# One run of matmuls for a unit's scores and the preceding unit's outputs, with the second head's blocks in the opposite rows

## The chip, the cores and the metric

One core of a Trainium2 chip runs the kernel. The time is device microseconds from start to end of one execution. The kernel before takes 614.58 us, the median of 3 runs (613.74 to 617.41).

## What is computed

Attention with a decay, in blocks of 64 positions (B = 4, H = 8 heads, S = 768, D = 64), and behind it a feed-forward net with softplus (512 to 2048 to 512) on all 3072 positions, in float32:

```
for b in range(nb):                                    # blocks of 64
    intra = (qb @ kb.T * Dmask) @ vb                   # Dmask[i,j] = lam**(i-j), 0 above the diagonal
    inter = (qb * lam_pow) @ kv_state
    out[b] = intra + inter
    kv_state = lam_block * kv_state + (kb * rev_pow).T @ vb
x = out laid out as (B*S, 512)
return softplus(x @ w_in) @ w_out
```

## The kernel before

The order of all instructions is written out by hand (`manual_schedule`): each engine runs its own in the order of the program, and waits are put in where data or buffers need them.

**Units.** The sequence is cut into 6 chunks of 128 positions, that is two blocks (s = 0 and 1) of 64. A *unit* g is one chunk of one pair of heads (t = 0 and 1) for all four batches b: 4 units to a chunk, 24 in all. Its q, k, v come in one buffer `att{g}` (two DMAs on SP, `load_upto`, L80 to L85). In SBUF block s = 0 stands in rows (partitions) 0 to 63, `lo`, and s = 1 in rows 64 to 127, `hi`.

For a unit, TensorE does two blocks of small fp32 matmuls (64 x 64 each):
- *scores* (`mm_scores`, L289 to L304): per b, t and s one product of k and q into the PSUM bank x, in rows `half(s)` (L299), and one of the decayed keys kd and v, the *sum* that the state takes up, into the bank y, in rows `half(1 - s)` (L301). In the last chunk the sums of s = 1 are left out.
- *outputs* (`mm_out`, L307 to L321): per b, s and t one product of state and decayed q (L314) and one of v and masked scores a (L318), into rows `half(t)` of bank s of a PSUM tile.

Around them: `k_decay` (ACT, two instructions, L277), `q_decay` (POOL for units under 8, VectorE after them, L284), `mask_scores` (VectorE, x times mask, into a, L326), `update_states` (VectorE, four instructions L331: from the state of block 0 to that of block 1, and on to the unit of the next chunk), `x_high` (ACT, L363) and `x_low` (VectorE, L370), which split a unit's outputs into two parts for the net.

**The net.** Step s of 96 takes 128 of the 2048 hidden columns of one chunk: 16 steps to a chunk. `mlp1(s)` (L389 to L401) is 12 matmuls of 128x128x512 into one PSUM bank (`bank`, L70, tag h, two buffers). `chain_act` (ACT, softplus, L379), `chain_hi` (ACT, L383) and `chain_lo` (VectorE, L387) make two parts of it. `mlp2(s - 4)` (L403 to L423), again 12 matmuls, adds the step into four banks of output rows. All matmuls of the net are in two parts, three products each.

**Weights.** They come as 64-bit numbers, and in the first chunk each step converts one pair of tiles: on ACT `w_scale`, `w_round` (L205, L209), on VectorE `w_shift`, `w_sign`, `w_add` (L213, L217, L223), and one step later `w_hi` on ACT (L226) and `w_lo` on VectorE (L230). `mlp2(s - 4)` and `mlp1(s)` need what `w_lo` made in step s - 1.

**Order.** A prologue written as a list of words (L453 to L463) does units 0 to 3 and the scores of unit 4, and the first steps. Then the loop from L473: in step s first the decays of the unit that has scores in step s + 1, then the chain of step s - 1, the weights, `mlp2(s - 4)`, a scores block if the step has one (steps 6, 9 and 12 for units 5 to 7, then 17, 21, ... 77), an outputs block if it has one (5, 8, 11, 14 for units 4 to 7, then 19, 23, ... 79), `mlp1(s)`, loads of weights, and, in a step with scores, the load of the next unit.

**Buffers.** PSUM has 8 banks: 4 for outputs of the net, 2 for h, 2 for the tile of the attention blocks (`work`, L66). In SBUF one pool of 21 buffers of 8 KB per row (`t8`) holds weights, raw weights, units, x parts, the `spare` tile of the prologue and the output rows; a tile waits until one is free. kd, qd and a of a unit are 2 KB tiles (`t2`, 4 buffers).

Of the kernel before, what the change touches and what calls it, by code (L numbers as in the profile page):

```python
# [7 lines left out]
F32 = mybir.dt.float32  # L8
# [3 lines left out]
ALU = mybir.AluOpType  # L12
# [4 lines left out]
T = 64  # L17
# [9 lines left out]
def half(i):  # L27
    return slice(i * 64, (i + 1) * 64)
# [3 lines left out]
def decay_attention_softplus_ffn(  # L32
# [19 lines left out]
        return sb.tile(shape, dt, tag="b4", bufs=7, name=name)  # L52

    def t2(shape, dt, name):
        return sb.tile(shape, dt, tag="b2", bufs=4, name=name)

    def tl(shape, dt, name):
        return sb.tile(shape, dt, tag="bl", bufs=1, name=name)
# [1 line left out]
    def th(shape, dt, name):  # L60
        return sb.tile(shape, dt, tag="bh", bufs=5, name=name)
# [5 lines left out]

        return ps.tile([128, 2, 512], F32, tag="t", bufs=1, name=name)

    def bank(name):  # L70
        return ps.tile([128, 512], F32, tag="h", bufs=2, name=name)

# [12 lines left out]
    def part(g, major, kind):  # L87
        return units[g][:, major, kind].rearrange("q (b t d) -> q b t d", b=B, t=2)
# [7 lines left out]
    def kt_of(g):  # L96
        return part(g, 1, 0)

    def vt_of(g):
        return part(g, 1, 1)  # L100


    w_order = [(f, 0) for f in range(LAG)]
# [27 lines left out]
    spare = t8([128, 4, 512], F32, "spare")  # L131
    warm = t8([128, 512], F32R, "warm")
    nc.vector.memset(warm.bitcast(F32), 0.0)
    warm_ps = bank("warm_ps")

    def keep_warm(n):
        for _ in range(n):
# [40 lines left out]
    nc.gpsimd.iota(  # L178
        off[half(1)], pattern=[[1, T]], base=0, channel_multiplier=-1, allow_small_or_imprecise_dtypes=True
    )  # L180
    diag = cp.tile([128, H, T], F32, name="diag")
    nc.vector.scalar_tensor_tensor(
        out=diag[half(1)], in0=off[half(1)].rearrange("q (o i) -> q o i", o=1).broadcast_to([64, H, T]), scalar=0.0,
        in1=lam_c[half(1)].rearrange("q (h o) -> q h o", o=1).broadcast_to([64, H, T]),
# [65 lines left out]
    def heads(g):  # L250
        p = g % NP
        return slice(2 * p, 2 * p + 2)

    def first_chunk(g):
        return g < NP

    def last_chunk(g):
        return g >= NG - NP
# [10 lines left out]
    def k_decay(g):  # L269
        kd = kds[g] = own(g, 0, "kd")  # L270
        if g == 0:
            w = rp1[:, heads(g)].rearrange("q (o t w) -> q o t w", o=1, w=1).broadcast_to([128, B, 2, D])
            nc.vector.tensor_mul(out=kd, in0=kt_of(g), in1=w)
            return
        for t in range(2):
            h = heads(g).start + t
            nc.scalar.activation(kd[:, :, t], kt_of(g)[:, :, t], AF.Copy, scale=rp1[:, h : h + 1])  # L277

    def q_decay(g):
        qd = qds[g] = own(g, 1, "qd")  # L280
        r = hi if first_chunk(g) else slice(0, 128)
        eng = nc.gpsimd if g < 2 * NP else nc.vector
        w = lp[r, heads(g), :].rearrange("q (o t) i -> q o (t i)", o=1).broadcast_to([r.stop - r.start, B, 2 * T])
        eng.tensor_mul(  # L284
            out=qd[r].rearrange("q b t i -> q b (t i)"), in0=q_of(g)[r].rearrange("q b t i -> q b (t i)"), in1=w
        )


    def mm_scores(g, x, y):  # L289
        q, k, kd, v = q_of(g), k_of(g), kds.pop(g), vt_of(g)  # L290
        if first_chunk(g):

            nc.tensor.matmul(y[lo], lhsT=warm[hi, :64], rhs=warm[hi], start=True, stop=False)
        for b in range(B):
            for t in range(2):
                cols = slice((2 * b + t) * 64, (2 * b + t + 1) * 64)
                for s in range(2):
                    r = half(s)
                    nc.tensor.matmul(x[r, cols], lhsT=k[r, b, t], rhs=q[r, b, t], start=True, stop=True)  # L299
                    if s == 0 or not last_chunk(g):  # L300
                        nc.tensor.matmul(  # L301
                            y[half(1 - s), cols], lhsT=kd[r, b, t], rhs=v[r, b, t],
                            start=s == 0 or not first_chunk(g), stop=s == 0 or not first_chunk(g),
                        )  # L304


    def mm_out(g, w):  # L307
        a, qd, v, st = aa.pop(g), qds.pop(g), vt_of(g), states[g]
        for b in range(B):
            cols = slice(b * 64, b * 64 + 64)  # L310
            for s in range(1 if first_chunk(g) else 0, 2):
                r = half(s)
                for t in range(2):
                    nc.tensor.matmul(w[half(t), s, cols], lhsT=st[r, b, t], rhs=qd[r, b, t], start=True, stop=False)  # L314
            for s in range(2):
                r = half(s)
                for t in range(2):
                    nc.tensor.matmul(  # L318
                        w[half(t), s, cols], lhsT=v[r, b, t], rhs=a[r, b, t],
                        start=s == 0 and first_chunk(g), stop=True,  # L320
                    )  # L321

    def mask_scores(g, x):
        a = aa[g] = own(g, 2, "a")
        m = mask[:, heads(g), :].rearrange("q (o t) i -> q o t i", o=1).broadcast_to([128, B, 2, T])
        nc.vector.tensor_mul(out=a, in0=x.rearrange("q (b t i) -> q b t i", b=B, t=2), in1=m)  # L326

    def decayed(g, to, of, r, u):
        for t in range(2):
            h = heads(g).start + t  # L330
            nc.vector.scalar_tensor_tensor(  # L331
                out=to[:, :, t], in0=of[:, :, t], scalar=lam_c[r, h : h + 1], in1=u[:, :, t],
                op0=ALU.mult, op1=ALU.add,
            )


    def first_states(g, y):
# [10 lines left out]
            )  # L348

    def next_states(g, y):  # L350
        nc.scalar.copy(out=states[g][lo].rearrange("q b t d -> q (b t d)"), in_=y[lo])

    def update_states(g, y):
        u = y.rearrange("q (b t e) -> q b t e", b=B, t=2)
        st = states[g]
        decayed(g, st[hi], st[lo], lo, u[hi])
        if not last_chunk(g):
            states[g + NP] = th([128, B, 2, D], F32, f"st_{g + NP}")
            decayed(g, states[g + NP][lo], st[hi], hi, u[lo])

    def x_high(g, w):

# [26 lines left out]
    def mlp1(s, ps_=range(NP)):  # L389
        c, f = divmod(s, NF)  # L390
        if s not in h_tiles:
            h_tiles[s] = bank(f"h{s}")
        w = w_of(f, 0)
        for p in ps_:
            cs = slice(p * 128, (p + 1) * 128)
            x = x_of(c, p)
            for n, (i, j) in enumerate(((0, 0), (1, 0), (0, 1))):
                nc.tensor.matmul(  # L398
                    h_tiles[s], lhsT=w[:, i, cs], rhs=x[:, j, :],
                    start=p == 0 and n == 0, stop=p == NP - 1 and n == 2,  # L400
                )  # L401

    def mlp2(ss):  # L403
# [6 lines left out]
        for b in range(B):  # L410
# [8 lines left out]
            if ends:  # L419
# [2 lines left out]
                queue = nc.scalar if c == NCH - 1 and b % 2 == 0 else nc.sync  # L422
                queue.dma_start(out=out[b * S + c * C : b * S + (c + 1) * C, :], in_=ob[:, b])  # L423

    def w_group(j):
        return (2 * j, 2 * j + 1) if 2 * j < NW else ()

    def scores_of(g):
        w = work(f"w{g}")
        mm_scores(g, w[:, 0], w[:, 1])  # L430
        mask_scores(g, w[:, 0])
        update_states(g, w[:, 1])


    xy, z = {}, {}
# [29 lines left out]
        step[name](*map(int, numbers))  # L465

    last = NCH * NF
    scores_at = {3 * n + 3: NP + n for n in range(NP)}  # L470
    scores_at.update({4 * n + 1 + NF: 2 * NP + n for n in range(NG - 2 * NP)})
    outs_at = {s + 2: g for s, g in scores_at.items()}
    for s in range(LAG, last + LAG):  # L473
        if s + 1 in scores_at:
            k_decay(scores_at[s + 1])
            q_decay(scores_at[s + 1])
        if s - 1 < last:
            chain_act(s - 1)
            chain_hi(s - 1)
            chain_lo(s - 1)  # L480
        old, new = w_group(s - 1), w_group(s)
        if old:
            w_hi(*old)
        if new:
            w_scale(*new)
            w_round(*new)
        if old:
            w_lo(*old)
        if new:
            w_shift(*new)  # L490
            w_sign(*new)
            w_add(*new)
        if s == last + LAG - 2:
            mlp2([s - LAG, s - LAG + 1])
        elif s - LAG < last - 1:
            mlp2([s - LAG])
        if s in scores_at:
            scores_of(scores_at[s])
        if s in outs_at:
            g = outs_at[s]  # L500
            w = work(f"z{g}")
            mm_out(g, w)
            x_high(g, w)
            x_low(g, w)
        if s < last:
            mlp1(s)
        w_load(2 * s + (8 if s < 9 else 6))
        if s in scores_at:
            load_upto(scores_at[s] + 2)


def _layout(q, k, v, lam, w_in, w_out):
    import numpy as np


    def split(a, back):
        a = a.reshape(B, NP, 2, NCH, 2, T, D).transpose(3, 1, 0, 2, 4, 5, 6)
        return a[:, :, :, :, :, ::-1] if back else a

    qs, ks, vs = split(q, False), split(k, True), split(v, True)  # L520

    dmaj = [a.transpose(0, 1, 4, 6, 2, 3, 5) for a in (qs, ks)]
    tmaj = [a.transpose(0, 1, 4, 5, 2, 3, 6) for a in (ks, vs)]
    att = np.stack([a.reshape(NCH, NP, 128, 512) for a in dmaj + tmaj], axis=3)
    att = np.ascontiguousarray(att).reshape(NCH, NP, 128, 2, 2, 512)
    wi = w_in.reshape(NP, 128, NF, 128).transpose(2, 1, 0, 3).reshape(NF, 1, 128, DM)
    wo = w_out.reshape(NF, 1, 128, DM)
    wts = np.ascontiguousarray(np.concatenate([wi, wo], axis=1)).view(np.int64)
    return att, np.ascontiguousarray(lam), wts
# [20 lines left out]
```

## Time and profile before

| | us |
|---|---|
| median of 3 runs | 614.58 (613.74 to 617.41) |
| the profiled execution | 615.21 |
| its span, first to last instruction | 613.4 |
| TensorE busy in it | 603.6 |
| VectorE, ACT busy in it | 227.0, 211.9 |

The profile is of one execution. Its rows give start and duration in microseconds on each engine; L with a number is a line of the kernel before. A row of the timeline joins neighbours of one kind (x12: twelve instructions, the duration being that of all together). PE is TensorE's matmuls, PEld its weight loads, DVE is VectorE, ACT is ScalarE, POOL is GpSimd, SP issues DMAs. What stands in brackets behind a row is the idle time of the engine before it and who ended it.

### The profile page before, as it was taken

How to read it: one execution, taken by the hardware profiler on the slowest of the kernel's cores; microseconds unless marked ns; L12 is line 12 of the kernel's file. 1: busy time of each engine (PE TensorE's matmuls, PEld its weight loads, DVE VectorE, ACT ScalarE, POOL GpSimd, SP SyncE). 2: the span in 40 equal slices, each digit the busy share in tenths (PEclk: the TensorE clock that was granted, in tenths of full speed). 3: DMA queues.
4: the chain of work that ended last, by engine and by line, in shares of the span. 5: the costliest groups of instructions: out<-in, count | busy, mean ns of one | idle time of the engine just before them, and what ended most of it. 6: DMA issues, size and time to landing. Idle time of an engine off the chain costs nothing.

```text
span 613.4 us, 11764 instructions
## 1 busy us (share of the span) xinstructions
PE 603.6 (98%) x5289; PEld 488.9 (80%) x5289; DVE 227.0 (37%) x330; ACT 211.9 (35%) x340; POOL 13.5 (2%) x17
## 2 busy tenths in 40 slices
PE   9899999999999999999999999999999999999997
PEld 6577778888888888888888888888888888888886
DVE  7679999843232223223213322222222211210111
ACT  3677677623222223132223231312312322322121
POOL 3200000000000000000000000000000000000000
PEclk9889999999999999999999999999999999999999
DMA  8995224213010032120030320002302000100001
GB/s 297 406 407 217 96 92 138 73 67 138 9 63 1 1 138 93 45 69 2 1 138 13 126 70 1 2 25 114 138 1 71 1 0 1 69 2 0 1 0 68
DMA packets 15169, 48.98 MB, mean 80 GB/s; under 512 B 1808, under 2 KB 1808, under 8 KB 15120
## 3 DMA queue, kind: packets, MB, share of 16 engines
q1 hardware_dynamic: 14832, 47.72, 21.3%
q8 instruction: 41, 0.67, 0.4%
q10 hardware_dynamic: 288, 0.52, 0.2%
q14 instruction: 8, 0.07, 0.0%
HBM read 41.95 MB, written 6.29 MB: 79 GB/s over the span
## 4 chain that ended last, share of the span: by engine, by line
PE 91%; DVE 3%; DMA 2%; ACT 1%; issue 1%; SPq 1%; POOL 0%; ACTq 0%; DVEq 0%
PE h L398 42%; PE o L415 41%; PE w L299 3%; PE z L314 2%; PE z L318 2%; DMA att<-in_att 2%; DVE w L230 1%; DVE st L331 1%; PE w L301 1%; DVE g L387 0%; ACT l L379 0%; ACT w L226 0%; DVE a L326 0%; SPq L84 0%; POOL own L284 0%
## 5 line engine op out<-in xcount | busy, mean ns | idle before, releaser
L398 PE MATMUL h<-x,w 128*128 128x512 f32 x1152 | 284.9, 396 | 0.0
L415 PE MATMUL o<-w,g 128*128 128x512 f32 x1152 | 277.1, 389 | 1.3 <-DVE w L230 1.3
L415 PEld LDWEIGHTS o<-w,g 128*128 128x128 f32 x1152 | 216.0, 188 | 47.3 <-DVE w L230 2.6
L398 PEld LDWEIGHTS h<-x,w 128*128 128x128 f32 x1152 | 213.9, 189 | 47.7 <-issue 0.8
L387 DVE TENSOR_TENSOR g<-l,g 128x512 fp32r<-128x512 f32 x96 | 66.4, 691 | 284.7 <-ACT g L383 284.6
L379 ACT ACTIVATE l<-h 128x512 f32<-128x512 f32 x96 | 57.3, 597 | 305.2 <-PE h L398 302.5
L383 ACT CAST g<-l 128x512 fp32r<-128x512 f32 x96 | 59.6, 621 | 3.1
L331 DVE SCALAR_TENSOR_TENSOR st<-st,lam_c,w 64x256 f32<-64x256 f32 x72 | 31.7, 479 | 0.8
L370 DVE TENSOR_TENSOR x<-z,x 128x512 fp32r<-128x512 f32 x24 | 16.6, 690 | 38.4 <-ACT x L363 38.4
L363 ACT CAST x<-z 128x512 fp32r<-128x512 f32 x24 | 14.0, 584 | 40.4 <-PE z L318 40.4
L299 PEld LDWEIGHTS w<-att 64*64 64x64 f32 x640 | 20.4, 134 | 7.0 <-issue 6.0
L326 DVE TENSOR_TENSOR a<-w,mask 128x512 f32<-128x512 f32 x20 | 13.8, 691 | 29.7 <-PE w L301 22.4
L299 PE MATMUL w<-att 64*64 64x64 f32 x640 | 23.1, 221 | 0.0
L301 PE MATMUL w<-att,kd 64*64 64x64 f32 x576 | 23.0, 221 | 0.0
L277 ACT ACTIVATE kd<-att,rp 128x256 f32<-128x256 f32 x40 | 18.1, 504 | 14.1 <-DMA att<-in_att 14.1
L230 DVE TENSOR_TENSOR w<-c,w 128x1024 fp32r<-128x1024 f32 (+1 forms) x19 | 21.1, 1112 | 4.7 <-ACT w L226 4.7
L314 PEld LDWEIGHTS z<-qd,st 64*64 64x64 f32 x640 | 17.0, 134 | 7.0 <-issue 7.0
L226 ACT CAST w<-c 128x1024 fp32r<-128x1024 f32 (+1 forms) x19 | 17.4, 914 | 15.0 <-DVE c L223 12.4
L205 ACT ACTIVATE c<-raw 128x1024 f32<-128x1024 f32 (+1 forms) x19 | 19.0, 999 | 7.4 <-DMA raw<-in_wts 7.4
L223 DVE CUSTOM_DVE_ANT_0 c<-raw,c 128x2048 uint16<-128x2048 uint16 (+1 forms) x19 | 20.1, 1057 | 2.4
L314 PE MATMUL z<-qd,st 64*64 64x64 f32 x640 | 20.9, 224 | 0.0
L301 PEld LDWEIGHTS w<-att,kd 64*64 64x64 f32 x576 | 20.3, 134 | 0.0
(47 smaller groups left out, 210.6 us busy)
## 6 DMA issues: line engine op xcount, KB each, us to landing
att<-in_att SPq DMA_DIRECT2D x48, 512.0 KB, 5.2
raw<-in_wts SPq DMA_DIRECT2D x32, 512.0 KB, 10.2
out_dram<-ob SPq DMA_DIRECT2D x22, 256.0 KB, 2.1
out_dram<-ob ACTq DMA_DIRECT2D x2, 256.0 KB, 2.0
lam_b<-in_lam SPq DMA_DIRECT2D x1, 4.0 KB, 2.6
```

Source lines behind the costliest of these rows:

```text
L205: nc.scalar.activation(c.bitcast(F32), raw_at(ks, 1).bitcast(F32), AF.Copy, scale=2.0**-112)
L223: nc.vector.tensor_add(out=c, in0=c, in1=raw_at(ks, 0))
L230: nc.vector.tensor_sub(out=w[:, 1], in0=conv.pop(ks[0]).bitcast(F32), in1=w[:, 0])
L299: nc.tensor.matmul(x[r, cols], lhsT=k[r, b, t], rhs=q[r, b, t], start=True, stop=True)
L301: nc.tensor.matmul(y[half(1 - s), cols], lhsT=kd[r, b, t], rhs=v[r, b, t], start=s == 0 or not first_chunk(g), stop=s == 0 or not first_ch ...
L314: nc.tensor.matmul(w[half(t), s, cols], lhsT=st[r, b, t], rhs=qd[r, b, t], start=True, stop=False)
L331: nc.vector.scalar_tensor_tensor(out=to[:, :, t], in0=of[:, :, t], scalar=lam_c[r, h : h + 1], in1=u[:, :, t], op0=ALU.mult, op1=ALU.add,)
L379: nc.scalar.activation(l_tiles[s], h_tiles.pop(s), AF.Softplus)
L383: nc.scalar.copy(out=g_tiles[s][:, 0, :], in_=l_tiles[s])
L387: nc.vector.tensor_sub(out=g[:, 1, :], in0=l_tiles.pop(s), in1=g[:, 0, :])
L398: nc.tensor.matmul(h_tiles[s], lhsT=w[:, i, cs], rhs=x[:, j, :], start=p == 0 and n == 0, stop=p == NP - 1 and n == 2,)
L415: nc.tensor.matmul(o_tiles[c][b], lhsT=g[:, i, b * 128 : (b + 1) * 128], rhs=w[:, j], start=f == 0 and n == 0, stop=f == NF - 1 and n == 2,)
```

## The change

A unit's scores and sums and the outputs of the unit before it are done in one function, `mm_both`, as one run of small matmuls: all outputs first, then `mm_sums`. There are 19 such runs (units 5 to 23: steps 6, 9, 12, 15, then 19, 23, ... 75); outputs of unit 23 remain a block of their own in step 79. Scores go into a bank of their own (tag z); the sums stand in columns 256 to 511 of the two banks in whose columns 0 to 255 the outputs are. From the second chunk on, the two blocks of the second head (t = 1) are stored in the opposite rows: `row(g, t, n)` says in which rows block n is. h has one buffer, and steps of `in_z` take the bank z for h instead. A copy of v (`keep_values`) lets a unit's buffer go before its outputs are done. `diag` moves into a part of `spare`, and its place goes to a fifth `t2` buffer.

```diff
-        return sb.tile(shape, dt, tag="b2", bufs=4, name=name)
+        return sb.tile(shape, dt, tag="b2", bufs=5, name=name)
-    def bank(name):
-        return ps.tile([128, 512], F32, tag="h", bufs=2, name=name)
+    def bank(name, tag):
+        return ps.tile([128, 512], F32, tag=tag, bufs=1, name=name)
+    def keep_values(g):
+        v = t2([128, B, 2, D], F32, f"v_{g}")
+        nc.scalar.copy(out=v, in_=part(g, 1, 1))
+        values[g] = v
-    diag = cp.tile([128, H, T], F32, name="diag")
+    diag = begins[0]
+    def row(g, t, n):
+        return n if first_chunk(g) else n ^ t
...
     def mm_scores(g, x, y):
...
+        u = y.rearrange("q (b t e) -> q b t e", b=B, t=2)
+        sums[g] = {(t, n): u[half(1 - row(g, t, n)), :, t] for t in range(2) for n in range(2)}
+        mm_sums(g, x, q, k, kd, v)
+
+    def mm_sums(g, x, q, k, kd, v):
         for b in range(B):
             for t in range(2):
                 cols = slice((2 * b + t) * 64, (2 * b + t + 1) * 64)
                 for s in range(2):
-                    r = half(s)
+                    r, n = half(s), row(g, t, s)
                     nc.tensor.matmul(x[r, cols], lhsT=k[r, b, t], rhs=q[r, b, t], start=True, stop=True)
-                    if s == 0 or not last_chunk(g):
...
+                    if n == 0 or not last_chunk(g):
+                        whole = n == 0 or not first_chunk(g)
+                        nc.tensor.matmul(sums[g][t, n][:, b], lhsT=kd[r, b, t], rhs=v[r, b, t], start=whole, stop=whole)
...
+    def mm_both(g, x, w):
+        q, k, kd, v = q_of(g), k_of(g), kds.pop(g), vt_of(g)
+        a, qd, vo, st = aa.pop(g - 1), qds.pop(g - 1), vt_of(g - 1), states[g - 1]
+        y = sums[g] = {}
+        for t in range(2):
+            for n in range(2):
+                s = row(g, t, n)
+                o = w[half(s), 0] if t else w[half(1 - s), 1]
+                y[t, n] = o[:, 256:512].rearrange("q (b e) -> q b e", b=B)
+        for b in range(B):
+            cols = slice(b * 64, (b + 1) * 64)
+            for n, (left, right) in enumerate(((st, qd), (vo, a))):
+                for s in range(2):
+                    r = half(s)
+                    for t in range(2):
+                        nc.tensor.matmul(
+                            w[half(t), row(g, t, s), cols], lhsT=left[r, b, t], rhs=right[r, b, t],
+                            start=n == 0, stop=n == 1,
+                        )
+        mm_sums(g, x, q, k, kd, v)
...
     def next_states(g, y):
-        nc.scalar.copy(out=states[g][lo].rearrange("q b t d -> q (b t d)"), in_=y[lo])
+        u = y[lo].rearrange("q (b t e) -> q b t e", b=B, t=2)
+        for t in range(2):
+            nc.scalar.copy(out=states[g][half(row(g + NP, t, 0)), :, t], in_=u[:, :, t])
...
+            h_tiles[s] = bank(f"h{s}", "z" if s in in_z else "h")
...
+    both_at = {3 * n + 6: NP + 1 + n for n in range(NP)}
+    both_at.update({4 * g - 17: g for g in range(2 * NP + 1, NG)})
+    in_z = {1, 3, 5} | {s + 1 for s in both_at} | {s - 1 for s in both_at if s > NF}
...
+        if s in both_at:
+            g = both_at[s]
+            w, xb = work(f"w{g}"), bank(f"x{g}", "z")
+            mm_both(g, xb, w)
+            x_high(g - 1, w)
+            x_low(g - 1, w)
+            mask_scores(g, xb)
+            update_states(g)
+            if NP + 1 < g < NG - 1:
+                keep_values(g)
+        if s == 4 * NG - 17:
+            zw = work(f"z{NG - 1}")
+            mm_out(NG - 1, zw)
+            x_high(NG - 1, zw)
+            x_low(NG - 1, zw)
         if s < last:
             mlp1(s)
         w_load(2 * s + (8 if s < 9 else 6))
-        if s in scores_at:
-            load_upto(scores_at[s] + 2)
+        if s in both_at:
+            load_upto(both_at[s] + 2)
...
     def split(a, back):
-        a = a.reshape(B, NP, 2, NCH, 2, T, D).transpose(3, 1, 0, 2, 4, 5, 6)
+        a = a.reshape(B, NP, 2, NCH, 2, T, D).transpose(3, 1, 0, 2, 4, 5, 6).copy()
+        a[1:, :, :, 1] = a[1:, :, :, 1, ::-1].copy()
```

`update_states` keeps its four VectorE instructions per unit, now on `sums[g]` and with rows by `row`; `mm_out` has the same products as before with `row` for the bank.

## Rows read from the trace of the kernel before

**Rows 1.** The page, parts 1 (busy us) and 2 (tenths in 40 slices)
```profile
PE 603.6 (98%) x5289; PEld 488.9 (80%) x5289; DVE 227.0 (37%) x330; ACT 211.9 (35%) x340; POOL 13.5 (2%) x17
...
DVE  7679999843232223223213322222222211210111
...
PEclk9889999999999999999999999999999999999999
```

**Rows 2.** TensorE's waits, 115 to 600 us: total, times, longest
```profile
PEld z L314 <- issue: 5.6, 16, 0.4
PEld w L299 <- issue: 5.6, 16, 0.4
```

**Rows 3.** TensorE's timeline around an output block: start, duration, what
```profile
106.34 2.88 PE L398 MATMUL h<-x,w 128*128 128x512 f32 x12
109.06 2.88 PE L415 MATMUL o<-w,g 128*128 128x512 f32 x12
...
112.04 0.30 PE L318 MATMUL z<-a,att 64*64 64x64 f32 x8
...
112.74 0.30 PE L318 MATMUL z<-a,att 64*64 64x64 f32 x8
112.97 3.02 PE L398 MATMUL h<-x,w 128*128 128x512 f32 x12
115.82 2.88 PE L415 MATMUL o<-w,g 128*128 128x512 f32 x12
```

**Rows 4.** TensorE's timeline, first passes of a scores block
```profile
129.51 0.27 PE L299 MATMUL w<-att 64*64 64x64 f32 x1
129.52 0.27 PE L301 MATMUL w<-att,kd 64*64 64x64 f32 x1
129.53 0.27 PE L299 MATMUL w<-att 64*64 64x64 f32 x1
129.53 0.27 PE L301 MATMUL w<-att,kd 64*64 64x64 f32 x1
```

**Rows 5.** TensorE's timeline in the prologue, outputs of unit 3
```profile
30.10 0.28 PE L318 MATMUL z<-own,att 64*64 64x64 f32 x4
30.22 0.28 PE L314 MATMUL z<-own,st 64*64 64x64 f32 x4
```

**Rows 6.** VectorE's timeline, steps 7 to 10
```profile
68.53 0.69 DVE L387 TENSOR_TENSOR g<-l,g 128x512 fp32r<-128x512 f32 x1
...
74.69 1.23 DVE L230 TENSOR_TENSOR w<-c,w 128x1024 fp32r<-128x1024 f32 x1 [0.51 <-ACT w L226]
...
79.06 0.68 DVE L370 TENSOR_TENSOR x<-z,x 128x512 fp32r<-128x512 f32 x1
...
81.46 1.79 DVE L213 TENSOR_SCALAR c<-c 128x1024 uint32<-128x1024 uint32 x1
...
85.80 0.68 DVE L326 TENSOR_TENSOR a<-w,mask 128x512 f32<-128x512 f32 x1
...
88.31 0.69 DVE L387 TENSOR_TENSOR g<-l,g 128x512 fp32r<-128x512 f32 x1
```

**Rows 7.** TensorE's timeline, steps 8 to 12
```profile
70.41 2.79 PE L415 MATMUL o<-w,g 128*128 128x512 f32 x11 [0.53 <-DVE w L230]
...
79.89 0.27 PE L299 MATMUL w<-att 64*64 64x64 f32 x1
...
86.56 2.88 PE L398 MATMUL h<-x,w 128*128 128x512 f32 x12
...
99.67 0.27 PE L299 MATMUL w<-att 64*64 64x64 f32 x1
...
100.77 3.02 PE L398 MATMUL h<-x,w 128*128 128x512 f32 x12
```

**Rows 8.** ACT's groups: busy us, mean ns, idle us before them and its end
```profile
L379 ACT ACTIVATE l<-h 128x512 f32<-128x512 f32 x96 | 57.3, 597 | 305.2 <-PE h L398 302.5 <-DVE g L387 2.6
...
L421 ACT COPY ob<-o 128x512 f32<-128x512 f32 x12 | 7.0, 586 | 9.2 <-PE o L415 9.2
```

## What I expect

> **What bounds the kernel now.** I read the page first, parts 1 and 2: TensorE is busy for 603.6 of 613.4 us, and its granted clock is full (tenths of 9, that is the 2.4 GHz level) from the fourth slice on; VectorE is full only in slices 4 to 7, about 46 to 107 us [rows 1]. A busy TensorE is not TensorE at its peak, so I read its waits next: between 115 and 600 us it waits for no other engine at all; the only rows are 0.35 us of its own issue, 16 times ahead of an output block and 16 times ahead of a scores block [rows 2]. So in four fifths of the span the end is set by what TensorE issues, and by nothing else. Third came TensorE's timeline. A layer run (12 matmuls of mlp1 or mlp2) takes 109.06 - 106.34 = 2.72 us. An output block stands between two of them: from the start of the run ahead of it to the start of the run behind it are 112.97 - 109.06 = 3.91 us, and that run then takes 2.85 [rows 3]. The block costs (3.91 - 2.72) + (2.85 - 2.72) = **1.32 us**. A scores block has as many products and costs the same: 100.77 - 99.67 = 1.10 us from its first pass to the next layer run [rows 7], and 1.09 in an output block. Fourth, VectorE's timeline for the stage where it is full, below.
>
> **Inside a block.** The 32 fp32 products of a block show as 64 passes, two each (L318 x8 where the code issues four). Four neighbours start within 0.02 us of each other: they are on four different quarters of the array, named here by input half and output half, 00, 01, 10, 11 [rows 4]. From L318 of b = 0 to L318 of b = 3 are 12 passes on each quarter: (112.74 - 112.04) / 12 = 0.0583 us a pass [rows 3]. Is that the price of a pass on one quarter, or of four passes through something they share? [rows 5] tells: in the prologue only the two quarters of one input half have work (four passes of L318, then four of L314, two on each), and 30.22 - 30.10 = 0.12 us go by for two passes each, again 0.06. So a quarter takes one pass in 0.058 us, whatever the other three do. So a block costs its fixed part plus the passes of its fullest quarter. Now that is 16 passes, 0.933 us; fixed part 1.32 - 0.933 = **0.387 us** (the first pass, and the change to and from whole-array matmuls).
>
> **The change, part by part.** *One run in place of two blocks.* 19 runs (units 5 to 23) and one last output block replace 19 scores and 20 output blocks; 19 fixed parts go, 19 x 0.387 = 7.35 us, were the passes the same. *But the quarters are no longer even.* In mm_both the outputs stay two per quarter and b: t goes to output half t. The sums don't: for head 0 they land in half(1-s), opposite the scores; for head 1 in half(s), the very quarter in which x[r] gets its scores. Per b, quarters 00 and 11 then have three products of mm_sums and 01 and 10 have one. The fullest has 4 x (2 + 3) = 20 products, 40 passes, 40 x 0.0583 = 2.333 us; a run costs 0.387 + 2.333 = **2.72 us**, against 2.64 for the two blocks. (In the last chunk, with n = 0 alone, quarter 11 still has three.) The merge loses 0.08 us each time. Bounds, since no row shows such a run: if only the total of passes counted, 0.387 + 32 x 0.0583 = 2.25; if products could start only in the program's order, one product more in the run, 2.84. I take 2.72, for [rows 5] is the nearest case: a part of the quarters in use, the pace unchanged.
>
> *The first stage, up to step 15.* Here VectorE decides [rows 6]. Its period of three steps, from one L387 after the states to the next, is 88.31 - 68.53 = 19.78 us; TensorE's, scores to scores, is 99.67 - 79.89 = 19.78 too [rows 7], though its own work is 6 x 2.72 + 2 x 1.32 = 18.96: the missing 0.82 is the wait of mlp2 at 70.41 for w_lo (L230). So what TensorE saves or pays here shows only through VectorE. VectorE's instructions stay (the long shift L213 of 1.79 us too), but their order doesn't: x_low (0.68 us at 79.06) moves from a step of its own into that of mask and states. Each step's L230 waits for ACT's w_hi, which waits for w_add; an attention operation in between covers this. Now only one step in three is uncovered (0.51 at 74.69); after it two are. Period 19.78 + 0.5 = 20.3. Nor is that the only place: bank z has the scores until mask_scores has read them, and then mlp1(s + 1). The mask ended at 85.80 + 0.68 = 86.48, mlp1(10) began at 86.56 [rows 6, 7]; with x_low ahead and 0.5 lost, the mask is 1.1 to 1.2 late and mlp1(10), which comes 0.7 later than now, waits some 0.4 us. This I count at nothing, since mlp2 behind it would have waited for L230 that long. If mask and w_lo didn't overlap so, it is the rival below.
>
> The run at step 6 begins 1.0 us earlier than scores(5) now (no output block at step 5: 1.32, less 0.3 for L230); two periods cost 0.5 each; so the run of unit 7 begins at about 99.7, as scores(7) do now, 99.67 [rows 7]. But unit 6's outputs, done by then before, are still in it. From here TensorE is the bound in both. Left before: 17 scores and 17 output blocks, 34 x 1.32 = 44.88 us. Left after: 17 x 2.72 + 1.32 = 47.56. Difference **+2.7 us**.
>
> *Costed at nothing, and what hides it.* keep_values: 17 copies on ACT at about 0.59 us (the copy of L421) beside 305 us in which ACT waits for mlp1 [rows 8]; uncovered, 10 us. With one bank each, h and z alternate; where two neighbours share h (steps 8 and 9, 77 to 95), mlp1 needs chain_act of the step before, 0.60 us, and has an mlp2 of 2.72 us to hide it. next_states: 4 copies become 8 half ones in the prologue, at most 4 x 0.6 more on ACT; I take 0 and keep 2 for the range. diag in begins[0] holds spare's buffer longer, while loads run far ahead: 0, up to 1. x_high now waits for the whole run, sums included; behind it on ACT stand keep_values and chain_act(s), whose mlp1 is only done 2.7 us later. Scores of a unit come two steps earlier, and its load_upto with its two DMAs on SP too, at steps 35, 51 and 67 now behind four output DMAs; a load still has three steps, over 16 us, until k_decay asks for it, and the copied values free its buffer sooner: 0.
>
> Sum on the profiled execution: 615.2 + 2.7 = 617.9; it was 0.6 above the median of the runs, so 617.3 against 614.58, +0.4%.
>
> **A rule that speaks against it.** In [rows 4] the two L299 products, from opposite input halves, write one bank and start 0.02 us apart. The Trainium skill, TensorEngine Tiling (Array Packing), Gotcha 1: PSUM Pressure, says that different row tiles cannot access the same PSUM bank at once. The trace disagrees with it. By that rule the new outputs, in which both input halves write each bank, would take turns: 16 passes more in 20 places, 18.7 us, and the time would be 636.
>
> **Rivals.** *Even pace* (only the number of passes counts): runs of 2.25, left after step 12 39.6 instead of 44.88, 609.3 us. For it: four quarters have only been seen evenly loaded; against it: [rows 5]. *VectorE's stage heals*: buffers come free earlier, so the waits like that at 70.41 go (there are three, at most 2.5 us together) and the periods don't grow: 19 x 0.08 - 2.5 = -1.0, 613.6 us. *Bank z holds TensorE* (slower): mlp1(s + 1) behind mask_scores at steps 6, 9, 12, 15. Each microsecond by which VectorE's list is later than in my walk is one of TensorE there, and a late mlp1 can make the next L387 late. At 1 us each, 4 more: 621.5; from 0.9 us each on it is over 1% slower. For it: VectorE has no slack from 46 to 107 us; against it: by the walk the wait for the mask and that for L230 lie one upon the other. *Banks taken in turn*: 636.
>
> **Chances.** Forecast 0.62, stage heals 0.13, even pace 0.09, bank z 0.14, banks in turn 0.02. A measurement of this kernel tells about 1%, 6.1 us. Forecast and healing lie within it, and half of the even pace: same 0.79; the other half, with some of the first stage won: faster 0.05; bank z and banks in turn: slower 0.16. The range, 612 to 622, leaves out the even pace and banks in turn, and takes in the 2.84 run (+2), next_states and the buffer.
>
> **What would show it.** Right: runs whose first pass stands about 2.49 us ahead of the next layer run (0.933 + 1.4 + 0.16), in whose last half two of four quarters fall idle; no TensorE wait after 125 us; the run of unit 7 at about 99.7; waits of k_decay gone. Wrong: runs of some 2.0 us, or waits of mlp1 for mask_scores of 1 us and more. A granted clock under full in the runs would break every term.

## The result: 621.4 us, ratio 1.010, and the profile after

The changed kernel takes 621.4 us (median of 4 runs, 620.06 to 621.7); the kernel before, in 4 runs, 614.16 (613.66 to 617.41). The ratio is 1.0099, with a 95% interval of 1.0071 to 1.0126: just about 1% slower, where 617.3 with a range of 612 to 622 was forecast. The profiled execution of after is 621.19 us with a span of 619.4, so 6.0 us more than the span of before.

The page of the kernel after, parts 1 and 2 (busy us; tenths in 40 slices), beside [rows 1]:

```profile
PE 610.0 (98%) x5289; PEld 499.1 (81%) x5289; DVE 227.2 (37%) x330; ACT 221.3 (36%) x361; POOL 13.3 (2%) x17
...
PEclk9689999999999999999999999999999999999999
```

TensorE still bounds the kernel, with the same 5289 matmuls, and is busy 6.4 us longer. Its granted clock has a dip in the second slice, deeper than before; that is the prologue, and it comes back below.

Waits of TensorE's weight loads in after, 115 to 600 us (total us, times, longest), beside [rows 2]:

```profile
PEld w L358 <- issue: 5.6, 16, 0.4
PEld z L336 <- issue: 0.4, 1, 0.4
PEld o L456 <- DVE w L239: 0.3, 1, 0.3
```

The 32 waits ahead of small matmuls are 17 now: 39 blocks of the loop have become 19 runs and one block, as the change says. The price of a run stands in TensorE's timeline around the run of unit 11 (start, duration, what), beside [rows 3]:

```profile
195.01 0.34 PE L358 MATMUL w<-qd,st 64*64 64x64 f32 x8
...
195.88 0.30 PE L358 MATMUL w<-a,v 64*64 64x64 f32 x8
196.00 0.22 PE L320 MATMUL x<-att 64*64 64x64 f32 x1
...
196.40 0.39 PE L320 MATMUL x<-att 64*64 64x64 f32 x7
196.58 0.33 PE L323 MATMUL w<-att,kd 64*64 64x64 f32 x7
...
197.54 3.03 PE L439 MATMUL h<-x,w 128*128 128x512 f32 x12
```

The outputs (L358, 64 passes) take 196.00 - 195.01 = 0.99 us; the scores and sums (L320, L323), 64 passes too, take 197.54 - 196.00 = 1.54. The second half is slower although it has as many passes. From the first pass to the next layer run are 2.53 us; 2.49 was forecast.

The first stage in after, TensorE's timeline (idle time and who ended it in brackets), beside [rows 7]:

```profile
81.45 0.34 PE L358 MATMUL w<-qd,st 64*64 64x64 f32 x8
...
86.85 2.88 PE L456 MATMUL o<-w,g 128*128 128x512 f32 x12
89.78 3.01 PE L439 MATMUL h<-x,w 128*128 128x512 f32 x12
...
93.60 2.79 PE L456 MATMUL o<-w,g 128*128 128x512 f32 x11 [0.59 <-DVE w L239]
...
101.90 0.34 PE L358 MATMUL w<-qd,st 64*64 64x64 f32 x8
```

and VectorE's over one period of it, beside [rows 6]:

```profile
71.28 0.69 DVE L428 TENSOR_TENSOR g<-l,g 128x512 fp32r<-128x512 f32 x1
...
77.45 1.23 DVE L239 TENSOR_TENSOR w<-c,w 128x1024 fp32r<-128x1024 f32 x1 [0.52 <-ACT w L235]
...
83.01 1.23 DVE L239 TENSOR_TENSOR w<-c,w 128x1024 fp32r<-128x1024 f32 x1 [0.51 <-ACT w L235]
...
88.35 0.69 DVE L411 TENSOR_TENSOR x<-w,x 128x512 fp32r<-128x512 f32 x1
88.95 0.68 DVE L367 TENSOR_TENSOR a<-x,mask 128x512 f32<-128x512 f32 x1
89.67 2.02 DVE L395 SCALAR_TENSOR_TENSOR st<-st,lam_c,w 64x256 f32<-64x256 f32 x4
91.72 0.69 DVE L428 TENSOR_TENSOR g<-l,g 128x512 fp32r<-128x512 f32 x1
```

The same four updates of the states in the kernel before:

```profile
86.49 1.79 DVE L331 SCALAR_TENSOR_TENSOR st<-st,lam_c,w 64x256 f32<-64x256 f32 x4
```

Two waits for w_hi (L235) of 0.5 us stand where [rows 6] have one, for x_low (L411) now follows in the step of mask and states. The four updates of the states take 2.02 us in place of 1.79. The period is 91.72 - 71.28 = 20.44 us, forecast 20.3.

**Where the 6 us are.** Steady stage first. From the run of unit 7 (before: the scores of unit 7, at 99.67) to the end of the span are 619.4 - 101.90 = 517.5 us, before 613.4 - 99.67 = 513.7: 3.8 us of the 6.0. The other 2.2 have arisen by the run of unit 7 (101.90 - 99.67). Most of them stand in the prologue, as the first mlp2 shows (L456, before L415). TensorE's clock beside it: the stretches' columns are length, busy time and count for PE, PEld, DVE, ACT and POOL, then the granted clock (of full, so 0.50 is the 1.2 GHz level), the DMA share and GB/s. After:

```profile
20.00:25.00 5.00, 5.00 (x75) 3.10 (x69) 3.54 (x6) 3.06 (x8) 0.59 (x1) 0.50 1.03 409
25.00:30.00 5.00, 5.00 (x112) 3.96 (x106) 2.40 (x5) 3.44 (x7) 1.28 (x1) 0.50 1.03 406
30.00:35.00 5.00, 5.00 (x55) 3.36 (x54) 1.32 (x3) 1.69 (x4) 1.27 (x1) 0.50 1.02 408
...
46.51 2.88 PE L456 MATMUL o<-w,g 128*128 128x512 f32 x12
```

Before:

```profile
20.00:25.00 5.00, 4.53 (x117) 3.40 (x114) 3.60 (x6) 3.60 (x7) 0.56 (x1) 0.87 1.03 406
25.00:30.00 5.00, 3.96 (x100) 2.55 (x96) 3.66 (x5) 4.05 (x7) 1.52 (x1) 1.00 1.03 408
30.00:35.00 5.00, 4.59 (x53) 3.61 (x48) 3.85 (x7) 3.46 (x7) 0.00 (x0) 0.66 1.03 408
...
44.53 2.88 PE L415 MATMUL o<-w,g 128*128 128x512 f32 x12
...
60.11 0.27 PE L299 MATMUL w<-att 64*64 64x64 f32 x1
```

From 20 to 35 us TensorE ran at half clock throughout in after, in before only in parts (0.87, 1.00, 0.66), and mlp2(0) is 46.51 - 44.53 = 1.98 us late. Two readings were possible: the new prologue is longer (half copies, `diag` in `spare`), or the clock was lower in this execution. The experiments have to tell them apart too.

### The profile page after: what moved, and what is told of

Its sections match the earlier page's. It is cut to its first block, busy times and chain, and to the rows that moved or that the text cites. A ratio compares the mean times of both kernels' runs of the same rounds, so it can differ in the third digit from the quotient of the medians.

```text
span 619.4 us, 11771 instructions
## 1 busy us (share of the span) xinstructions
PE 610.0 (98%) x5289; PEld 499.1 (81%) x5289; DVE 227.2 (37%) x330; ACT 221.3 (36%) x361; POOL 13.3 (2%) x17
## 4 chain that ended last, share of the span: by engine, by line
PE 84%; DMA 8%; DVE 5%; ACT 1%; issue 1%; SPq 0%; DVEq 0%; ACTq 0%
PE o L456 39%; PE h L439 38%; DMA raw<-in_wts 7%; PE w L358 3%; PE x L320 2%; PE w L323 2%; DMA att<-in_att 1%; DVE c L232 1%; DVE c L226 1%; DVE st L395 1%; DVE c L222 0%; DVE g L428 0%; DVE w L239 0%; ACT c L214 0%; ACT w L235 0%
## 5 line engine op out<-in xcount | busy, mean ns | idle before, releaser
L456 PE MATMUL o<-w,g 128*128 128x512 f32 x1152 | 278.0, 390 | 1.5 <-DVE w L239 1.5
L456 PEld LDWEIGHTS o<-w,g 128*128 128x128 f32 x1152 | 215.6, 188 | 48.7 <-DVE w L239 4.3
L320 PE MATMUL x<-att 64*64 64x64 f32 x736 | 34.9, 228 | 0.0
L320 PEld LDWEIGHTS x<-att 64*64 64x64 f32 x736 | 32.5, 141 | 1.3 <-issue 0.9
L411 DVE TENSOR_TENSOR x<-w,x 128x512 fp32r<-128x512 f32 x19 | 13.1, 690 | 52.6 <-ACT x L404 52.5
L323 PE MATMUL w<-att,kd 64*64 64x64 f32 x576 | 31.3, 227 | 0.0
L404 ACT CAST x<-w 128x512 fp32r<-128x512 f32 x19 | 11.1, 584 | 54.3 <-PE w L323 54.3
L323 PEld LDWEIGHTS w<-att,kd 64*64 64x64 f32 x576 | 25.8, 134 | 0.0
L235 ACT CAST w<-c 128x1024 fp32r<-128x1024 f32 (+1 forms) x19 | 17.4, 914 | 15.8 <-DVE c L232 15.7
L239 DVE TENSOR_TENSOR w<-c,w 128x1024 fp32r<-128x1024 f32 (+1 forms) x19 | 21.2, 1114 | 4.4 <-ACT w L235 4.2
L358 PEld LDWEIGHTS w<-qd,st 64*64 64x64 f32 x608 | 16.1, 134 | 6.7 <-issue 6.7
L226 DVE SCALAR_TENSOR_TENSOR c<-raw,c 128x1024 uint32<-128x1024 uint32 (+1 forms) x19 | 21.0, 1107 | 0.6
L358 PE MATMUL w<-qd,st 64*64 64x64 f32 x608 | 19.8, 224 | 0.0
L218 ACT ACTIVATE raw<-raw 128x1024 uint32<-128x1024 uint32 (+1 forms) x19 | 18.8, 988 | 0.0
```

Of the source, the lines that this page charges most:

```text
L226: nc.vector.scalar_tensor_tensor(out=c, in0=raw_at(ks, 1), scalar=0x80000000, in1=c, op0=ALU.bitwise_and, op1=ALU.bitwise_or)
L239: nc.vector.tensor_sub(out=w[:, 1], in0=conv.pop(ks[0]).bitcast(F32), in1=w[:, 0])
L323: nc.tensor.matmul(sums[g][t, n][:, b], lhsT=kd[r, b, t], rhs=v[r, b, t], start=whole, stop=whole)
L358: nc.tensor.matmul(w[half(t), row(g, t, s), cols], lhsT=left[r, b, t], rhs=right[r, b, t], start=n == 0, stop=n == 1,)
L456: nc.tensor.matmul(o_tiles[c][b], lhsT=g[:, i, b * 128 : (b + 1) * 128], rhs=w[:, j], start=f == 0 and n == 0, stop=f == NF - 1 and n == 2,)
```

## The experiments

Theory: a run costs a fixed part and the passes of its fullest quarter, so 40 passes where 32 would do if the quarters were even; what is lost ahead of it lies in the order on VectorE and in the clock of the prologue. Rivals: the mere number of passes counts; the move of x_low costs nothing; the prologue's edits are what delays it.

**Taking passes from the full quarters, or from the idle ones.** From unit 5 on, the sums of one head are left out, and the update uses the other head's in their place (the lines that do this are not shown): of t = 1 (quarters 00 and 11, the full ones) or of t = 0 (01 and 10).

```diff
+                        if g <= NP or t != 1:      # second kernel: t != 0
                             nc.tensor.matmul(sums[g][t, n][:, b], lhsT=kd[r, b, t], ...)
```

> Leaves out the sums of the second head (t = 1) in the 19 merged runs; update_states takes those of the first head in their place, so that the work behind is the same and the output is not. These are the products that stand on quarters 00 and 11, which have scores too. Theory (the fullest quarter sets a run): the fullest falls from 20 products to 16, a run from first pass to the next layer run goes from 2.53 to 2.06 us, the whole to about 613 us. Rival (the number of passes counts, whatever quarter): 16 of 128 passes fewer, at four to a round 0.23 us, runs of 2.29, about 617 us.

> Leaves out the sums of the first head (t = 0) instead, as many products, from quarters 01 and 10, which have 12 of them against 20; update_states takes those of the second head. Theory (fullest quarter): the fullest keeps its 20, a run stays at 2.53 us and the whole at about 621 us, though an eighth of the passes is gone. Rival (number of passes): runs of 2.29, about 617 us, as in the other kernel.

TensorE's timeline without the sums of t = 1, one run and the layer run behind it (this view ends before the last two of its 12 matmuls):

```profile
191.73 0.34 PE L361 MATMUL w<-qd,st 64*64 64x64 f32 x8
...
193.76 2.56 PE L442 MATMUL h<-x,w 128*128 128x512 f32 x10
```

and without those of t = 0:

```profile
195.22 0.34 PE L361 MATMUL w<-qd,st 64*64 64x64 f32 x8
...
197.75 3.03 PE L442 MATMUL h<-x,w 128*128 128x512 f32 x12
```

Both runs have 112 passes in place of 128. The first takes 2.03 us, the second 2.53, exactly what the whole run takes. 16 passes taken from the idle quarters are worth nothing, 16 from the full ones 0.50 us: eight passes on each, 0.063 apiece. The times, of one execution each, point the same way: 611.4 and 621.4 us. Of the 10.0 us between them 2.0 stand ahead of the run of unit 7 (100.15 and 102.14 us), where the second had the lower clock in the prologue; 8.0 stand behind it. So it is the fullest quarter, and not the number of passes.

**x_low one step later.** In steps 7, 10, 13 and no longer in the step of mask and states:

```diff
+        if s - 1 in (6, 9, 12):
+            x_low(*late)
...
-            x_low(g - 1, w)
...
+            late = (g - 1, w)
```

> x_low of units 5 to 7 is put back into the step after the run (steps 7, 10, 13), behind that step's w_add, as it stood alone before; in the run's own step VectorE does mask and states first. Theory (VectorE sets the first stage, and x_low in the step of mask and states costs one uncovered wait for w_hi per period and holds the mask): the period from run to run in the first stage falls from 20.4 to about 19.8 us, mlp1 no longer waits for mask_scores, the whole falls by about 1.5 us to 619.8. Rival (the stage is longer only because the runs are): no change, 621.4.

First passes of the runs of units 6 and 7 in TensorE's timeline:

```profile
78.57 0.34 PE L358 MATMUL w<-qd,st 64*64 64x64 f32 x8
...
98.42 0.34 PE L358 MATMUL w<-qd,st 64*64 64x64 f32 x8
```

The period is 19.85 us, where after has 20.45 and before 19.78. The time is 617.81 us (617.34 to 619.93, 10 runs), ratio to before 1.0042 (1.0019 to 1.0066). So the order on VectorE is what lengthens the first stage, and that can be had back without touching the run. (This profile had full clock in the prologue, so the time as a whole holds more than the two periods' 1.2 us. Executions of like clock compare better: with a mean clock of 0.988 or 0.989 this kernel takes 619.2 to 619.9 us in three, the changed kernel 621.2 to 621.7 in three.)

**Even quarters.** Outputs placed so that the sums of t = 1 fall on the half-empty quarters, with the sums of t = 0 first. Both halves of the array would then write the same rows of a bank in one run, so a small copy on ACT orders outputs and sums (no run here leaves it out):

```diff
-                o = w[half(s), 0] if t else w[half(1 - s), 1]
+                o = w[half(1 - s), 1 - t]
...
+        nc.scalar.copy(out=fence, in_=w[:, 0, 255:256])
         mm_sums(g, x, q, k, kd, v)
```

> The quarters are evened out: the second head's sums go to half(1 - s) as the first's do, all products of t = 0 come ahead of those of t = 1, and a small ACT copy of one column of the outputs orders the two (a bank half is written by one input half at a time). Every quarter has 16 products. Theory (fullest quarter): a run from first pass to the next layer run is 2.06 us if the copy is done in time, up to 0.5 more if TensorE waits for it; the whole 613.5, at most 620. Rival (number of passes): no change, 2.53 and 621.4, or more with the copy.

Waits in this kernel from 130 to 600 us:

```profile
PEld w L324 <- ACT fence L363: 4.8, 15, 0.3
...
PE w L324 <- ACT fence L363: 2.7, 15, 0.2
```

In these 15 runs the time from the first pass to the layer run is 2.53 us, as in after: TensorE stands still for the copy ahead of the first sum. If even quarters bring the 0.47 us that were expected, as much is lost here. In the first stage it is worse: 3.14 to 3.82 us a run, with the copy behind w_scale and w_round on ACT. 621.1 us (619.29 to 624.59), ratio 1.0095 (1.0066 to 1.0125). By itself this kernel does not tell the theories apart; the next one does.

**Even quarters, with cover for the copy.** The sums of t = 0 don't touch what the copy guards. Here only those of t = 1 wait for it, and only units 9 to 23 are placed anew; the order of the sums, t = 0 first, holds for all units:

```diff
+                o = w[half(1 - s), 1 - t] if g > 2 * NP or not t else w[half(s), 0]
...
+        f = nc.scalar.copy(out=fence, in_=w[:, 0, 255:256]) if g > 2 * NP else None
...
+                        if f is not None and t == 0:
+                            tc.declare_no_dep(m.ins, f.ins, reason="another bank")
```

> The changed kernel, in units 9 to 23 alone with outputs of t placed so that the t = 1 sums fall on the quarters that are half empty: every quarter then has 16 products (32 passes) instead of 20 or 12. The price is a small copy on ACT between outputs and sums, for which only the sums of t = 1 wait; those of t = 0 go on meanwhile. Theory (a run costs its fixed part and the passes of its fullest quarter, 0.0583 us each): from the first pass to the next layer run 2.526 - 8 x 0.0583 = 2.06 us in these 15 runs, so 15 x 0.47 = 7.0 us less than the changed kernel, about 613 to 615 by the clock in the prologue. Rival (the total of 128 passes counts, not the fullest quarter): 2.5 us and 620 to 621.5. Rival (the copy still holds the matmuls): a wait for ACT of 0.1 to 0.4 us in each run, 2.2 to 2.4 us, 616 to 619.

> As e5_even3, and x_low of units 5 to 7 put one step later, as in e3_xlate. Theory: the two edits lie in different stretches and add up. First-stage period 19.85 us in place of 20.45, runs of unit 5 to 7 still 2.53 us, runs of units 9 to 23 2.06 us: e3_xlate's 617.8 less 7.0, 610.8 us, and 609 to 612 by the clock in the prologue; that is under the kernel before. Rival (the later stage takes back what the first gains, since something else, buffers or loads, sets its pace): not under 613.

> As e6_even3_xlate, and 12 further matmuls, whose result nobody reads, put into the prologue where TensorE idles, after the first three mlp groups. Theory (mlp2(0) starts at 42 us or at 46.7 according to how long TensorE's granted clock was at half before it, 0 to 17 us, and that depends on how busy TensorE was): the granted clock stays full from 18 to 37 us, mlp2(0) starts at 42 to 43 us, the span is 0 to 2 us under that of e6_even3_xlate and its spread over the runs smaller. Rival (the half clock comes and goes whatever TensorE does here): half clock again in the profile, the same median as e6_even3_xlate. Rival (the further matmuls stand in the way): mlp2(0) later with full clock, slower by up to 2 us.

> The changed kernel once more, beside the others of this call. Theory: 620 to 621.5 us, runs of 2.53 us, first-stage period 20.45; the start of mlp2(0) follows the time that the granted clock was at half between 18 and 37 us: 42 with none, 44 with 4 us, 46.5 with 15 us. Rival (the new copies of next_states and the place of diag delay the prologue): mlp2(0) at 46.5 whatever the clock.

The timeline of the first of these four, around the run of unit 11:

```profile
192.34 0.34 PE L361 MATMUL w<-qd,st 64*64 64x64 f32 x8
...
193.57 0.16 ACT L365 COPY fence<-w 128x1 f32<-128x1 f32 x1 [2.59 <-PE w L361]
...
194.40 3.03 PE L443 MATMUL h<-x,w 128*128 128x512 f32 x12
```

and around the run of unit 7, which has the new order of the sums, but the old placing (this view ends before the last six matmuls of the layer run):

```profile
100.16 0.34 PE L361 MATMUL w<-qd,st 64*64 64x64 f32 x8
...
102.68 1.65 PE L443 MATMUL h<-x,w 128*128 128x512 f32 x6
```

The copy ends at 193.73, while the sums of t = 0 are still going on, and nothing waits. The run of unit 11 takes 2.06 us with all 128 passes; 2.06 was forecast. That of unit 7 takes 2.52, so the new order alone brings nothing. In units 9 to 23 this kernel differs from the one with the copy ahead of all sums only in what waits for the copy: 2.06 and 2.53 us, so the uncovered copy cost 0.47. The time is 612.22 us (610.91 to 614.58, 10 runs), the changed kernel beside it 621.39 (618.95 to 622.2, 5 runs), before 617.16 (613.56 to 618.62, 14 runs). From the run of unit 7 (100.16 in the one, 101.88 in the other) to the end are 510.4 and 517.5 us: 7.1 less, forecast 7.0. The rest of the difference lies ahead of that run.

With x_low late as well: 609.95 us (609.88 to 610.04, 4 runs), ratio to before 0.9905 (0.9871 to 0.9939). Its timeline:

```profile
77.86 0.34 PE L361 MATMUL w<-qd,st 64*64 64x64 f32 x8
...
97.71 0.34 PE L361 MATMUL w<-qd,st 64*64 64x64 f32 x8
```

The period is 19.85 again, and from there to the end 608.2 - 97.71 = 510.5 us. The two edits add up. This version is faster than both kernels, though the ratio flatters it: its four executions had full clock, and those of before beside them a mean clock of 0.982 to 1. The two of before with 0.997 or more take 613.56 and 613.95 us, so that some 4 us (0.6%) are the edits'.

With 12 further matmuls in the prologue on top: 609.66 us (609.51 to 609.76, 4 runs), ratio 0.99 (0.9866 to 0.9933). mlp2(0) starts at 41.38 in place of 42.03, of which 0.3 us are left in the medians. All 4 runs had full clock, but so had all 4 of the kernel without these matmuls, so this pair says nothing on the clock. Nor do the further executions of the changed kernel settle the prologue alone: the profiled one has half clock again from 25 to 35 us, and mlp2(0) again at 46.5.

**The clock of the prologue.** The same 12 matmuls in the kernel before and in the changed one:

```diff
-... a 1, mlp 0 0, sl 0, ...      mlp 0 1, load 8, ...              mlp 0 2, add 3, ...
+... a 1, mlp 0 0, warm 5, sl 0, ...  mlp 0 1, warm 3, load 8, ...  mlp 0 2, warm 4, add 3, ...
```

> The kernel before with the 12 further matmuls, whose result nobody reads, in the prologue as in e7_even3_xlate_warm. Theory (in the prologue TensorE's granted clock falls to half after stretches in which TensorE had little to do, and each execution has its own luck): the clock stays full in every run, the runs lie within 1 us of each other, at 612.5 to 613.5 us, where the kernel before itself ranges from 613.4 to 618.6. Rival (the half clock comes whatever TensorE does here): the same spread and median as the kernel before.

> The changed kernel with the same 12 further matmuls. Theory: the clock stays full, the runs lie within 1 us, at 616.5 to 617.5 us. With the clock out of the way the difference to e9_before_warm is what the edit itself costs: unit 6's outputs left over 1.32, 17 runs of 2.767 in place of 2.64 make 2.16, later waits 0.44 and the first stage 0.25, together 4.2 us; mlp2(0) starts in both within 0.5 us of 41.4. Rival (the half copies of next_states and the place of diag cost something in the prologue): mlp2(0) of the changed kernel 1 to 2 us later than in e9_before_warm, and a difference of 5 to 6 us.

Windows and timelines (TensorE, VectorE) of before with these matmuls:

```profile
30.00:35.00 5.00, 4.56 (x48) 3.60 (x48) 3.25 (x7) 3.70 (x8) 0.00 (x0) 1.00 1.02 407
...
42.70 2.88 PE L415 MATMUL o<-w,g 128*128 128x512 f32 x12
...
98.44 0.27 PE L299 MATMUL w<-att 64*64 64x64 f32 x1
...
34.79 0.42 DVE L213 TENSOR_SCALAR c<-c 128x512 uint32<-128x512 uint32 x1
...
43.11 0.69 DVE L387 TENSOR_TENSOR g<-l,g 128x512 fp32r<-128x512 f32 x1
```

and of the changed kernel with them:

```profile
30.00:35.00 5.00, 5.00 (x51) 3.76 (x50) 3.59 (x6) 4.20 (x9) 1.23 (x1) 1.00 1.03 407
...
42.16 3.08 PE L456 MATMUL o<-w,g 128*128 128x512 f32 x12
...
99.23 0.34 PE L358 MATMUL w<-qd,st 64*64 64x64 f32 x8
...
34.25 1.49 DVE L222 TENSOR_SCALAR c<-c 128x512 uint32<-128x512 uint32 x1
...
43.76 0.69 DVE L428 TENSOR_TENSOR g<-l,g 128x512 fp32r<-128x512 f32 x1
```

The mean clock of the whole execution is 0.997 or more in all 14 runs of the two; the kernel before, beside them, had 0.982 to 0.997 in 13 runs. Before with these matmuls takes 614.0 us (613.68 to 614.35, 10 runs), without them 615.02 (613.52 to 618.37, 13 runs): the spread is gone, and the best runs are no better. The changed kernel with them takes 618.82 us (618.51 to 619.22).

At equal clock the changed kernel's mlp2(0) starts 0.54 us *earlier* (42.16 against 42.70), so that it was the clock that made mlp2(0) late. (Both stand later than the 41.4 expected.) But VectorE, which sets the next stage, comes out of the prologue 0.65 us *later*: the chain_lo ahead of the loop's first w_shift starts at 43.76 against 43.11. It was 0.54 ahead at the w_shift shown (34.25 against 34.79), which then takes 1.49 us in place of 0.42. POOL works beside it, as its 1.23 us from 30 to 35 show: it is q_decay of unit 4, at 33.77, which in before stands at 40.08 us. In all ten profiles with the changed prologue it starts between 32.9 and 33.8 us, in the two with the old one at 40.1 and 41.9. So the change brings this q_decay forward; that it is what makes the instruction longer is read from this pair of traces, and no run tests it.

At equal clock the edit costs 618.82 - 614.0 = 4.8 us of time, 616.7 - 612.2 = 4.5 of span, a little more than the 4.2 expected. Both kernels came out 0.5 to 2.3 us above what was expected of them: the first stage gives back a part of an earlier start. In the kernel before, mlp2(0) came 1.83 us earlier with these matmuls (42.70 against 44.53), the scores of unit 7 only 1.23 (98.44 against 99.67).

## Why the prediction was right, and where it was short

621.4 us lie in the range of 612 to 622, 0.6 under its upper end. Between the medians are 7.2 us, where 2.7 were forecast; with the 12 matmuls in both kernels 4.8 are left, so some 2.4 are the clock in the prologue, for which the forecast had no term. The room up to 622 was made for other things (a run of 2.84 us, next_states, the buffer); that it sufficed is partly luck. The number is also that of the rival in which bank z holds TensorE (621.5), but the trace does not show that rival's waits, as said below.

The sum of the prediction beside the two profiled executions, and beside the pair at equal clock (us of span, changed kernel minus before):

| part | predicted | as profiled | both with the 12 matmuls |
|---|---|---|---|
| up to mlp2(0) | 0 | 1.98 | -0.54 |
| mlp2(0) to the run of unit 7 | 0 | 0.25 | 1.33 |
| unit 6's outputs still in that run | 1.32 | 1.32 | 1.32 |
| 17 runs against 17 pairs of blocks | 1.36 | 2.02 | 2.02 |
| waits behind the run of unit 7 | 0 | 0.44 | 0.44 |
| sum | 2.7 | 6.0 | 4.6 |

**Right: the run costs more than the two blocks.** This was the step that decided the sign. "The fullest has 4 x (2 + 3) = 20 products" holds: the two kernels with a head's sums left out show it, and the even quarters show it a second time, with all the work in. With even quarters 17 runs would take 17 x 0.47 = 8 us less than they do, and the kernel would have been faster than before.

**Mis-sized: the run, 2.72 predicted, 2.77 measured.** In after (means over the runs) 0.092 us pass ahead of the first pass, 2.526 to the layer run, and that run takes 0.149 longer than an undisturbed one: 2.767. The four runs of the last chunk take 2.49 instead of 2.53. So 13 x 0.127 + 4 x 0.092 = 2.0 us for the runs, in place of 17 x 0.08 = 1.4. Of the missing 0.05, 0.036 lie inside the run: 24 passes more than a block at 0.0583 would make 1.092 + 1.399 = 2.491. Without the sums of t = 1 the run is 2.025, exactly a block and 16 passes; the extra comes with those sums. What it is, the runs don't show.

**Right in kind, somewhat short in size: the stage of VectorE.** The second uncovered wait for w_hi is there, 0.52 and 0.51 us, and the period is 20.44, forecast 20.3. "VectorE's instructions stay" was not quite so: the four updates of the states take 0.23 us more. Counted from mlp2(0), the run of unit 5 comes at 61.01 - 46.51 = 14.50 where the scores of before come at 60.11 - 44.53 = 15.58: 1.08 earlier, forecast 1.0. Two periods give back 1.33, forecast 1.0. So the run of unit 7 is 0.25 late in this stage. It was to stand at 99.7, and stands at 101.90 because of the prologue. At equal clock the agreement is less close: with VectorE 0.65 late from the prologue, the run of unit 5 comes only 0.50 us ahead of the scores of before (58.35 against 58.85), two periods give back 1.29, and the run of unit 7 is 0.79 late (99.23 against 98.44), where 0 was forecast.

**Right: bank z.** mlp1(10) can start once the mask has been read: the mask ends at 88.95 + 0.68 = 89.63, and mlp1(10) starts at 89.78, 0.2 after mlp2(6) would have let it (86.85 + 2.72 = 89.57). "some 0.4 us" was forecast, hidden by the wait for w_lo (L239) behind it. That wait, 0.8 to 0.9 us per period, is still there, so nothing came of the rival with 1 us each.

**Failed: "next_states ... I take 0", and with it a prologue taken as fixed.** The half copies do not delay mlp2(0) at equal clock, but VectorE leaves the prologue 0.65 us late there, with q_decay of unit 4 beside its work on weights; the prediction had no term for it. And the prediction read the clock of one execution ([rows 1] have slices under full in the prologue) and made the sum against that execution, as if the next one would have the same. It had not: half clock from 20 to 35 us, 1.98 us. The prediction named a clock under full in the runs as what would break it, and did not think of the prologue. At equal clock the difference of the two profiles is 4.5, not 6.0. Whether the change makes the half clock more frequent stays open: of nine executions of the changed kernel none has a mean clock of 0.997 or more, of 46 of the kernel before 13; but the kernel with x_low one step later, whose prologue is that of the changed kernel, has 1.0 in 3 of 10.

**Failed: no wait behind the run of unit 7.** "no TensorE wait after 125 us" holds, yet two small ones stand ahead of that, in steps 14 and 15, 0.31 and 0.13 us for w_lo. The prediction had TensorE as the bound from the run of unit 7, step 12, on.

**Banks in turn.** In after both input halves write outputs into each of the two banks, and eight passes, two on each quarter, take 196.00 - 195.88 = 0.12 us, as two on each of two quarters did in [rows 5]; a run is 2.53 us. The Trainium skill, TensorEngine Tiling (Array Packing), Gotcha 1: PSUM Pressure, says that different row tiles cannot access the same bank at the same time; the measurement disagrees, and decides.

## What to carry to other kernels

Small matmuls on quarters of the array cost what the fullest quarter has, so count products per quarter before merging two blocks: the merge saves a fixed part of 0.4 us, and eight passes too many on one quarter, 0.47 us, eat it. If an order has to be put between two parts of such a run, give TensorE matmuls in between that don't need it; the same copy cost 0.47 us a run without such a cover, and no wait shows with it. And before a difference of 1% between two profiles is put down to an edit, compare the granted clock stretch by stretch; a few matmuls that nobody reads made the executions comparable here.

## What the runs showed of the hardware

- The clock of a stretch differs between executions of one kernel. In kernels with the changed prologue and without the 12 matmuls, mlp2(0) starts at 42.03 and 42.72 with no half clock from 20 to 35 us, at 44.03 and 43.35 with some (0.66 in one of three windows; 0.51 and 0.80 in two) and at 46.51, 46.52 and 46.73 with most or all of it. The next stage, where VectorE decides, takes a part of that back: the changed kernel's mlp2(0) came 4.35 us earlier with the 12 matmuls, its end 2.7. TensorE was not idle when the clock was at half (busy 5.00 of 5.00 us in each of the three windows of after); what sets off the fall in one execution and not in another stays open.
- The four quarters do not keep to one order among themselves. In after, seven passes of L320 in a row start at 196.40, ahead of the L323 passes at 196.58, where the program has the two lines in turn, two passes each. The Trainium skill, TensorE: Matmul & The Clock Gate, Part 3: Packing small matmuls, says that matmuls start and end in the order of the program; here the rows show otherwise.
